# Seventy products of zeros among the first three head pairs, PSUM buffers for phi and its way back, and a split placed two units later

## The chip, the cores and the metric

The kernel runs on one core of one Trainium2 chip. The metric is the time of one execution on the device in microseconds (us). A core has TensorE (PE: matmuls and transposes, results go to PSUM), VectorE (DVE), ScalarE (ACT), GpSimd (POOL), SyncE (SP), which issues most DMAs here, and 16 DMA engines. Each engine works through its own instructions in order; between engines they wait on semaphores.

## The reference

Three layers, each fed by the one before:

```python
# attention: 4 batches, 8 heads, 576 tokens, 64 per head; blocks of 64
scores = scale * np.matmul(q, k.transpose(0, 1, 3, 2))
mask = block_i >= block_j
scores = np.where(mask, scores, -1000000000.0)
attn = softmax(scores)            # exp(s - max) / (sum + 1e-09)
out = np.matmul(attn, v)          # as x: 2304 tokens of 512
# a layer with a bend
h = x @ w_in                      # 512 -> 2048
g = np.where(pos, h, np.where(neg, 0.0, (h + beta) ** 2 / (4.0 * beta)))
x = g @ w_out                     # 2048 -> 512
# soft mixture: 8 experts of 4 slots
logits = x @ phi                  # 512 -> 32
d = softmax(logits, over tokens); slot_input = d.T @ x
slot_out[e] = np.maximum(slot_input[e] @ w1[e], 0.0) @ w2[e]
c = softmax(logits, over slots);  return c @ slot_out
```

## The kernel before

**Attention.** Sixteen units of work, one for each batch and pair of heads ("pair" 0 to 15). A string, PLAN, lists the steps of six overlapping pairs for one round; rounds follow each other, so it sets the order of instructions. For a pair and a group i of query rows (i = 4, 3, ... 0, two blocks of 128 rows each), `sc` i is six matmuls of scores into a PSUM tile of two banks (L120; L113 for i = 4), `mk` i adds the mask with two small matmuls (L126), `mx` takes the negative row maxima on DVE (L146, tile `nm`), `ex` the exponentials on ACT (L151, tile `pr`), `no` scales them on POOL (L163), `pt` transposes them on PE (L171), `pc` copies the result out (L254 on ACT, or DVE), and `pv` multiplies by the values (L189, L194). Score tiles have two buffers (pool `psc`), so `sc` of one group waits until ACT has read the group before the last. In this phase POOL, ACT and DVE also prepare the first seven tiles of `w_in` (READY).

**Split products.** `h = x @ w_in` is computed in three terms with both operands split into a high and a low part. A tile w of `w_in` takes a chain: raw data by DMA, `w_mul` on ACT (L460), four steps of `w_bits` on DVE (L466 to L469, tile `wab`), the cast of the high part on ACT (L254), then two steps on POOL (L484 and L485) that leave the low part in `w`. Inputs x are split by block of tokens: `split` casts on ACT (L409, `xh`) and subtracts on POOL (L412, `xl`).

**The layer after attention** (`Moe.run`). UNITS lists (block, tile) in order; unit k is twelve matmuls L538 into a tile `h` (pool `ptr`, tag "tr", three buffers; transposes of attention use the same group), followed by the bend: for even k below 18 three steps on ACT (L561, L562, L564), for odd k one on ACT (L559) and one on DVE (L572), then L573 on DVE for both, which reads `h` last and so frees it. The units here are k = 0 (block 1, tile 4), 1 (1, 5), 2 (1, 6), 3 (0, 7), 4 (1, 7), 5 (0, 8), 6 (1, 8), 7 (0, 9); w7 is needed at k = 3, w8 at 5, w9 at 7. In the loop, before unit k's matmuls, come `w_parts` of one weight (cast and POOL steps), `w_mul` and `w_bits` of another, and at k = 1 `parts[1]`, the second half of the split of block 2.

**The weight `w_out`, folded with phi.** The transposes `wo_turn` (L498), `wo_phi` (L507: 32 matmuls of a turned tile with `phi`, and an ACT copy to `y`, L511) and `wo_back` (L516: one transpose, and an ACT copy to `w2p`, L517) all write one bank, `aside[:, 1]`, the second bank of a tile kept from `psc`. There are four `phi` and four returns, in places that a planner lays (the four `phi` begin at 276.96, 298.80, 321.96 and 346.22 us); each stands after the third quarter of a unit's matmuls (`mid` in `h_unit`) or behind a unit.

**Tail.** Soft mixture and experts, with expert weights streamed in by DMAs whose issues wait for buffers. Here 25 products of zeros (`gap`, L1015) stand between dependent steps; 44 others (`warm`, L30) open the program.

Of the kernel before, what the change touches and what calls it, by code (L numbers as in the profile page):

```python
# [7 lines left out]
F32 = mybir.dt.float32  # L8
# [6 lines left out]
P = 128  # L15
# [223 lines left out]

FILL = ""  # L240
WARM = 44

# [3 lines left out]
def attention(e, tc, nb=4, wl=(1, 1 + 2 * READY)):  # L248
    nc = tc.nc
    e.ENG = ENG  # L250

    def copy(eng, dst, src):
        if eng == "A":
            nc.scalar.copy(dst, src)  # L254
        elif eng == "D":
            nc.vector.tensor_copy(dst, src)
        else:
            nc.gpsimd.tensor_scalar(out=dst, in0=src, scalar1=1.0, scalar2=1.0, op0=ALU.mult, op1=ALU.mult)
    e.copy = copy
    e.eng = lambda c: nc.vector if c == "D" else nc.gpsimd  # L260

    e.QD, e.pr, e.v_, e.acc = [], [], [], []
    for i in range(2):
        e.QD.append(e.apool.tile([P, 2, P], F32R, tag=f"QD{i}", bufs=1, name=f"QD{i}"))
        z = (nc.gpsimd, nc.vector)[i]
        z.memset(e.QD[i][0:64, :, 64:P].bitcast(F32), 0.0)
        z.memset(e.QD[i][64:P, :, 0:64].bitcast(F32), 0.0)
        e.pr.append([e.apool.tile([P, P * (b // 2 + 1)], F32, tag=f"pr{i}{b}", bufs=1, name=f"pr{i}{b}")
                     for b in range(9)])
        z.memset(e.pr[i][8][:, 576:640], 0.0)  # L270
        e.v_.append(e.apool.tile([P, 5, 2, 64], F32, tag=f"natv{i}", bufs=1, name=f"vn{i}"))
        z.memset(e.v_[i][64:P, 4], 0.0)
    for i in range(2):
        e.acc.append(e.apool.tile([P, 16, 2], F32, tag=f"acc{i}", bufs=1, name=f"ac{i}"))
        nc.vector.memset(e.acc[i], 1e-9)
    e.low = e.apool.tile([P, P], mybir.dt.bfloat16, tag="low", bufs=1, name="low")
    e.one = e.apool.tile([P, 64], mybir.dt.bfloat16, tag="one", bufs=1, name="one")
    nc.vector.memset(e.low, 0.0)
    nc.vector.memset(e.one, 1.0)
    for h in (0, 64):  # L280
        nc.vector.memset(e.low[h:h + 1, 0:64], -2.0 ** 127)
    pairs = [Pair(e, nc, b, p) for b in range(nb) for p in range(4)]
    n = len(pairs)
    plan = [(it - int(u[0]), u[1:]) for it in range(n + 6) for u in PLAN.split()]
    plan = [(i, u) for i, u in plan if ((i, int(u[2:])) in EARLY if u[0] == "h" and u[1] in "mxyzoa" else
                                        0 <= i < n if u[0] != "w" else wl[0] <= i < wl[1])]
    fill = [(int(u[0]), u[1:]) for u in FILL.split()]
    assert sorted(fill) == sorted(plan[:len(fill)])
    for i, u in fill + plan[len(fill):]:
        if u[0] == "h":  # L290
            e.moe.early(u[1], *EARLY[i, int(u[2:])])
        elif u[0] != "w":
            pairs[i].step(u)
        else:
            t, c = (i - wl[0]) // 2, slice((i - wl[0]) % 2 * 256, (i - wl[0]) % 2 * 256 + 256)
            if u == "w0" and c.start == 0:
                e.moe.w_raw(t)
            elif u == "w1":
                e.moe.w_mul(t, c)
                e.moe.w_bits(t, c)  # L300
            elif u == "w2":
                e.moe.w_parts(t, c, e.ENG["w"])
# [14 lines left out]
class Moe:  # L317
# [183 lines left out]

    def wo_phi(self, c):
        e, nc = self.e, self.nc
        ps = self.aside[:, 1]
        for kk in range(4):
            for i in range(4):
                nc.tensor.matmul(ps[32 * i:32 * i + 32, 0:P], e.phi[:, kk], self.wT[2 * c + i // 2][:, i % 2, kk],  # L507
                                 start=(kk == 0), stop=(kk == 3))
        self.drop(f"wT{4 * c}", f"wT{4 * c + 2}")
        wp = self.wp = e.y[:, 3]  # L510
        nc.scalar.copy(wp, ps[:, 0:P])  # L511

    def wo_back(self, c):
        e, nc = self.e, self.nc
        ps = self.aside[:, 1]
        nc.tensor.transpose(ps[:, 0:P], self.wp, e.ident)  # L516
        nc.scalar.copy(e.w2p[:, 4 * c:4 * c + 4].rearrange("p i s -> p (i s)"), ps[:, 0:P])  # L517

# [374 lines left out]
    def run(self):  # L893
        if not self.dry:
            d = Moe(Null(), Null(), self.live)
            d.home, d.w = dict(self.home), dict.fromkeys(range(READY), Null())
            d.xw = dict.fromkeys(self.xw, Null())
            d.xt = dict.fromkeys(self.xt, Null())
            d.g = dict.fromkeys(self.g, Null())
            d.run()  # L900
            self.plan, self.middle, self.bend = d.tape, d.middle, d.bend
            self.ends = {k: t for t, k in enumerate(d.tape) if isinstance(k, tuple)}
            self.cap = sum(self.CAP.values())
            self.tape = []
        self.gn, self.v, self.S = {}, {}, {}
        units = self.UNITS
        at, prep = self.plan_sides({u: k for k, u in enumerate(units)})
        e, nc = self.e, self.nc
        self.aside = e.psc.tile([P, 2, 512], F32, tag="sc", name="aside")
        self.lt = {1: self.aside[:, 0]}  # L910
        for i in range(READY, READY + 2):
            self.w_raw(i)
        self.w_mul(READY)
        self.w_bits(READY)
        parts = list(self.split(2))
        parts[0]()
        for k, (b, f) in enumerate(units):
            for i in [READY + n for n, p in enumerate(prep) if p == k - 1]:
                self.w_parts(i)
            for i in [READY + n for n, p in enumerate(prep) if p == k > 0]:  # L920
                self.w_mul(i)
                self.w_bits(i)
            if k == 1:
                parts[1]()
            for i in [READY + n for n, p in enumerate(prep) if max(p - 2, 0) == k and n > 1]:
                self.w_raw(i)
            self.h_unit(b, f, at.pop(-k, ()) if k else ())
            self.act_unit(b, f, "D" if k > prep[-1] or k < 18 and k % 2 else "A")
            for fn, *a in at.pop(k, []):
                (getattr(self, fn) if isinstance(fn, str) else fn)(*a)  # L930
            if k == 66:
                self.n4 = self.new([P, 4, 256], F32R, "n4")
                for i in range(4):
                    self.comb_parts(i)
            if k == 57:
                self.middle, self.spare = len(self.tape), 1
            if k > 29:
                self.feed()
        assert not at
        self.bend = len(self.tape)  # L940
        self.spare = 0
        self.chain()
        self.tail()
# [301 lines left out]
```

## Time and profile before

| what | value |
|---|---|
| median of 3 runs | 523.71 us (523.31 to 523.95) |
| the profiled execution | 523.28 us, of which 521.5 are the span of instructions |
| mean granted clock of PE | 0.98 of full speed |
| PE busy | 500.6 us, 96% |
| DVE, ACT, POOL busy | 331.6, 327.0, 203.9 us |
| moved by DMA | 91.01 MB, mean 175 GB/s |

The profile is one execution on the hardware. Busy times of PE are modelled at their ends, since matmuls are pipelined. "Idle before, releaser" names what ended the idle time ahead of an instruction. The granted clock is in parts of 2.4 GHz; 0.50 is 1.2 GHz. PEld is the loading of weights into PE, which overlaps with matmuls.

### The profile page before, as it was taken

The numbers are of one execution on the slowest core, as the hardware profiler recorded it, in microseconds if no ns is written. First come the engines' busy times: TensorE is split into PE (matmuls) and PEld (weight loads), VectorE is DVE, ScalarE is ACT, GpSimd is POOL, SyncE is SP. The second block draws the span as 40 slices with busy tenths as digits, with TensorE's granted clock in tenths as the row PEclk, the third lists the DMA queues.
The fourth block names the chain that finished last, engine by engine and source line by source line (L and its number), as shares of the span: only waits on it lengthen the run. The fifth ranks groups of instructions, "written<-read, shape, count | busy, mean of one in ns | idle before, by whom it ended". The sixth has DMA issues, their size and how long they took to land.

```text
span 521.5 us, 11780 instructions
## 1 busy us (share of the span) xinstructions
PE 500.6 (96%) x4504; PEld 384.5 (74%) x4504; DVE 331.6 (64%) x672; ACT 327.0 (63%) x734; POOL 203.9 (39%) x264
## 2 busy tenths in 40 slices
PE   6799999999999999899999999899999999999994
PEld 5678887888888887688887887788767978753453
DVE  6879988888887655888888545833463444431232
ACT  4889998888887645557787888643333535452131
POOL 3888997777777424744523212600002000000000
PEclk8789999999999999899999999999999999999998
DMA  6235334343321155111257865341075679979997
GB/s 204 92 95 167 115 99 142 88 125 98 91 52 29 53 163 215 53 43 61 101 168 236 288 235 184 110 154 41 5 277 175 222 253 412 391 237 373 411 412 308
DMA packets 42711, 91.01 MB, mean 175 GB/s; under 512 B 8736, under 2 KB 18080, under 8 KB 42656
## 3 DMA queue, kind: packets, MB, share of 16 engines
q1 hardware_dynamic: 42656, 90.26, 51.0%
q8 instruction: 36, 0.59, 0.4%
q14 instruction: 19, 0.16, 0.1%
HBM read 74.51 MB, written 14.68 MB: 171 GB/s over the span
## 4 chain that ended last, share of the span: by engine, by line
PE 81%; ACT 4%; DMA 3%; DVE 3%; issue 1%; POOL 1%; SPq 0%; ACTq 0%; DVEq 0%; POOLq 0%
PE h L538 33%; PE sc L120 7%; PE gn L593 5%; PE om L189 5%; PE s L658 3%; PE eh L1031 3%; PE ps_1p L171 2%; PE sc L113 2%; PE lt L613 2%; PE ps_2p L171 2%; PE ps_3p L171 2%; PE acc L1058 2%; PE om L194 2%; PE ps_0p L171 2%; DMA ew<-in_w2b_dram 1%
## 5 line engine op out<-in xcount | busy, mean ns | idle before, releaser
L538 PE MATMUL h<-xh,w 128*128 128x512 f32 (+1 forms) x384 | 115.2, 368 | 0.0
L538 PE MATMUL h<-xt,w 128*128 128x512 f32 x384 | 101.2, 408 | 1.6 <-POOL w L485 1.4
L163 POOL TENSOR_SCALAR pr<-pr,sm 128x512 f32<-128x512 f32 (+2 forms) x144 | 88.7, 633 | 24.7 <-DVE sm L158 23.0
L151 ACT ACTIVATE pr<-sc,nm 128x512 f32<-128x512 f32 (+2 forms) x144 | 78.3, 551 | 10.1 <-DVE nm L146 8.6
L538 PEld LDWEIGHTS h<-xt,w 128*128 128x128 f32 x384 | 69.5, 191 | 16.2 <-POOL w L485 2.7
L572 DVE SCALAR_TENSOR_TENSOR g<-g 128x512 f32<-128x512 f32 (+1 forms) x52 | 37.6, 724 | 65.6 <-ACT g L559 65.6
L538 PEld LDWEIGHTS h<-xh,w 128*128 128x128 f32 x384 | 69.0, 189 | 13.8 <-issue 3.8
L538 PE MATMUL h<-xl,w 128*128 128x512 f32 (+1 forms) x192 | 68.1, 355 | 0.0
L146 DVE TENSOR_REDUCE nm<-sc 128x2 f32<-128x1024 f32 (+1 forms) x64 | 52.3, 818 | 21.2 <-PE sc L126 20.9
L573 DVE TENSOR_TENSOR g<-h,g 128x512 f32<-128x512 f32 (+1 forms) x80 | 50.9, 636 | 15.8 <-ACT g L564 13.7
L559 ACT ACTIVATE g<-h,half 128x512 f32<-128x512 f32 (+1 forms) x52 | 32.3, 622 | 43.1 <-PE h L538 41.5
L120 PE MATMUL sc<-K,Q 64*128 64x512 f32 (+3 forms) x384 | 47.8, 363 | 3.7 <-ACT pr L151 2.7
L689 POOL TENSOR_TENSOR cn<-cn,cm 128x128 f32<-128x128 f32 (+1 forms) x5 | 1.9, 378 | 124.7 <-DVE cm L688 124.7
L254 ACT COPY gn<-gn 128x1024 f32<-128x1024 f32 x35 | 35.3, 1009 | 13.1 <-PE gn L593 12.7
L120 PEld LDWEIGHTS sc<-K,Q 64*128 64x128 f32 x384 | 30.2, 196 | 14.0 <-issue 5.6
L538 PEld LDWEIGHTS h<-xl,w 128*128 128x128 f32 x192 | 36.4, 189 | 3.8
L477 POOL TENSOR_TENSOR wab<-wab 128x512 f32<-128x512 f32 x16 | 21.0, 1312 | 44.0 <-DVE wab L469 23.3
L593 PE MATMUL gn<-ident,g 128*128 128x128 f32 x280 | 36.7, 274 | 0.2 <-ACT gn L254 0.2
L593 PEld LDWEIGHTS gn<-ident,g 128*128 128x128 f32 x280 | 31.7, 140 | 6.7 <-issue 2.1
L484 POOL TENSOR_TENSOR wab<-wab,w 128x256 f32<-128x256 f32 (+1 forms) x23 | 23.2, 1010 | 22.5 <-ACT w L254 21.3
L467 DVE SCALAR_TENSOR_TENSOR wab<-wab 128x512 uint32<-128x512 uint32 (+1 forms) x39 | 25.4, 651 | 10.0 <-ACT wab L460 6.6
L561 ACT ACTIVATE g<-h,half 128x512 f32<-128x512 f32 x28 | 19.3, 689 | 19.9 <-PE h L538 15.8
(226 smaller groups left out, 892.1 us busy)
## 6 DMA issues: line engine op xcount, KB each, us to landing
ew<-in_w_dram SPq DMA_DIRECT2D x32, 512.0 KB, 6.8
raw<-in_w_in_dram SPq DMA_DIRECT2D x16, 512.0 KB, 5.3
raw<-in_w_out_dram SPq DMA_DIRECT2D x16, 512.0 KB, 4.3
ew<-in_w2a_dram SPq DMA_DIRECT2D x16, 510.0 KB, 8.8
ew<-in_w2b_dram SPq DMA_DIRECT2D x16, 344.0 KB, 6.7
kn<-in_k_dram SPq DMA_DIRECT2D x16, 288.0 KB, 3.2
qn<-in_q_dram SPq DMA_DIRECT2D x16, 288.0 KB, 4.3
vn<-in_v_dram SPq DMA_DIRECT2D x16, 256.0 KB, 3.3
```

The source lines that it names most:

```text
L120: nc.tensor.matmul(sc[:, h, 0:n], self.Q[r, qa, 128 * i:128 * i + 128], self.K[r, ka, 0:n], start=(k == 0), stop=False)
L146: nc.vector.tensor_reduce(out=self.negm[:, 2 * i:2 * i + 2], in_=self.scs[i][:, :, 0:128 * (i + 1)], axis=AX.X, op=ALU.max, negate=True)
L151: self.nc.scalar.activation(pr, sc, AF.Exp, bias=self.negm[:, b:b + 1], accum_out=self.acc[:, b, 0:1])
L163: self.nc.gpsimd.tensor_scalar(out=pr, in0=pr, scalar1=self.sums[:, b:b + 1], scalar2=1.0, op0=ALU.mult, op1=ALU.mult)
L171: nc.tensor.transpose(ps[:, u * P:(u + 1) * P], self.pr[b][:, kc * P:(kc + 1) * P], e.ident)
L189: nc.tensor.matmul(om[64 * h:64 * h + 64, (t0 - ts[0]) * P:len(ts) * P], self.v[:, kc, h, :], self.PT[:, a:a + 2 * n - 1:2], start=(kc == ...
L254: nc.scalar.copy(dst, src)
L538: nc.tensor.matmul(ph[:, 0:n], w[:, wi, kk], self.x(b, kk, xi)[:, 0:n], start=(kk + m == 0), stop=(kk + m == 5))
L559: nc.scalar.activation(g, ph, AF.Relu, bias=e.half[:, 0:1], scale=0.5)
L572: nc.vector.scalar_tensor_tensor(out=g, in0=g, scalar=1.0, in1=g, op0=ALU.min, op1=ALU.mult)
L573: nc.vector.tensor_tensor(out=g, in0=ph, in1=g, op=ALU.max)
L593: nc.tensor.transpose(ps[:, j, i * P:(i + 1) * P], self.gt(b, f)[:, o:o + P], e.ident)
```

## The change

It does three things.

First, a table KEEP gives for ten `mk` steps of pairs 0, 1 and 2 a number of 128x128 products of zeros (bf16, the constant tile that `warm` uses too), 70 in all: 28 in pair 0, 27 in pair 1 and 15 in pair 2. They stand right behind the `mk` step on PE, write into a new tile of the "tr" group each, and nothing reads them.

Second, `wo_phi` and `wo_back` take a tile of the "tr" group each (`ph`, `bk`) and write there; `wo_turn` stays in `aside[:, 1]`.

Third, `parts[1]` is called at unit k = 3 where it was called at k = 1.

```diff
--- before.py
+++ after.py
@@ -239,6 +239,8 @@
 
 FILL = ""
 WARM = 44
+KEEP = {(0, "mk2"): 20, (0, "mk1"): 6, (0, "mk0"): 2, (1, "mk3"): 6, (1, "mk2"): 6, (1, "mk1"): 13, (1, "mk0"): 2,
+        (2, "mk3"): 5, (2, "mk2"): 5, (2, "mk1"): 5}
 
 
 
@@ -291,6 +293,10 @@
             e.moe.early(u[1], *EARLY[i, int(u[2:])])
         elif u[0] != "w":
             pairs[i].step(u)
+            if (i, u) in KEEP:
+                keep = e.ptr.tile([P, 512], F32, tag="tr", name=f"keep{i}{u}")
+                for _ in range(KEEP[i, u]):
+                    nc.tensor.matmul(keep[:, 0:P], e.zero, e.zero, start=True, stop=True)
         else:
             t, c = (i - wl[0]) // 2, slice((i - wl[0]) % 2 * 256, (i - wl[0]) % 2 * 256 + 256)
             if u == "w0" and c.start == 0:
@@ -501,7 +507,7 @@
 
     def wo_phi(self, c):
         e, nc = self.e, self.nc
-        ps = self.aside[:, 1]
+        ps = e.ptr.tile([P, 512], F32, tag="tr", name=f"ph{c}")
         for kk in range(4):
             for i in range(4):
                 nc.tensor.matmul(ps[32 * i:32 * i + 32, 0:P], e.phi[:, kk], self.wT[2 * c + i // 2][:, i % 2, kk],
@@ -512,7 +518,7 @@
 
     def wo_back(self, c):
         e, nc = self.e, self.nc
-        ps = self.aside[:, 1]
+        ps = e.ptr.tile([P, 512], F32, tag="tr", name=f"bk{c}")
         nc.tensor.transpose(ps[:, 0:P], self.wp, e.ident)
         nc.scalar.copy(e.w2p[:, 4 * c:4 * c + 4].rearrange("p i s -> p (i s)"), ps[:, 0:P])
 
@@ -920,7 +926,7 @@
             for i in [READY + n for n, p in enumerate(prep) if p == k > 0]:
                 self.w_mul(i)
                 self.w_bits(i)
-            if k == 1:
+            if k == 3:
                 parts[1]()
             for i in [READY + n for n, p in enumerate(prep) if max(p - 2, 0) == k and n > 1]:
                 self.w_raw(i)
```

Lines of the kernel after stand 2 lower from L239 on and 6 lower behind attention's loop (L484 is L490, L412 is L418, L498 is L504, and so on).

On POOL, from the first half of block 2's split to the third of the weights that follow. Before (`xl_3054` and `xl_3081` are the halves; `w_3076`, `w_3130` and `w_3175` are w7, w8 and w9):

```order
L412 TENSOR_TENSOR xl_3054<-xw_148,xh_3053 128x512 x2
L484 TENSOR_TENSOR wab_3047<-wab_3047,w_3076 128x512
L485 TENSOR_TENSOR w_3076<-wab_3047 128x512
L412 TENSOR_TENSOR xl_3081<-xw_149,xh_3080 128x512 x2
L484 TENSOR_TENSOR wab_3101<-wab_3101,w_3130 128x512
L485 TENSOR_TENSOR w_3130<-wab_3101 128x512
L484 TENSOR_TENSOR wab_3150<-wab_3150,w_3175 128x512
L485 TENSOR_TENSOR w_3175<-wab_3150 128x512
```

And after (in the same order w7, w8 and w9 are `w_3156`, `w_3205` and `w_3255`, the second half `xl_3210`):

```order
L418 TENSOR_TENSOR xl_3134<-xw_148,xh_3133 128x512 x2
L490 TENSOR_TENSOR wab_3127<-wab_3127,w_3156 128x512
L491 TENSOR_TENSOR w_3156<-wab_3127 128x512
L490 TENSOR_TENSOR wab_3176<-wab_3176,w_3205 128x512
L491 TENSOR_TENSOR w_3205<-wab_3176 128x512
L418 TENSOR_TENSOR xl_3210<-xw_149,xh_3209 128x512 x2
L490 TENSOR_TENSOR wab_3230<-wab_3230,w_3255 128x512
L491 TENSOR_TENSOR w_3255<-wab_3230 128x512
```

The second `xl` has gone from ahead of w8's two steps to behind them, ahead of w9's.

On ACT, from the cast of w7 to that of w8. Before:

```order
L254 CAST w_3076<-wab_3047 128x512
L409 CAST xh_3080<-xw_149 128x1024
L559 ACTIVATE g_4_3071<-h_5_3085,half 128x512
L460 ACTIVATE wab_3101<-raw_3045 128x512
L561 ACTIVATE g_6_3122<-h_6_3109,half 128x512
L562 ACTIVATE g_6_3122<-g_6_3122,unit 128x512
L564 ACTIVATE g_6_3122<-g_6_3122 128x512
L254 CAST w_3130<-wab_3101 128x512
```

And after:

```order
L256 CAST w_3156<-wab_3127 128x512
L565 ACTIVATE g_4_3151<-h_5_3160,half 128x512
L466 ACTIVATE wab_3176<-raw_3125 128x512
L567 ACTIVATE g_6_3197<-h_6_3184,half 128x512
L568 ACTIVATE g_6_3197<-g_6_3197,unit 128x512
L570 ACTIVATE g_6_3197<-g_6_3197 128x512
L256 CAST w_3205<-wab_3176 128x512
L415 CAST xh_3209<-xw_149 128x1024
```

The second cast `xh` has gone from ahead of the bend of unit 1 (its L559) to behind the cast of w8; the bends and `w_mul` (L460, then L466) keep their order among each other.

On PE, the matmuls between the first `phi` and the turn of a weight after it, with the semaphores on which they wait (each named by the engine that raises it). Before:

```order
L507 MATMUL aside<-wT_3552,phi 32x128 x2
L507 MATMUL aside<-wT_3612,phi 32x128 x2
L538 MATMUL h_4_3685<-xh_3080,w_1619 128x512
L538 MATMUL h_4_3685<-xl_3081,w_1619 128x512
L538 MATMUL h_4_3685<-xh_3080,w_1619 128x512
L498 MATMUL aside<-ident,wab_3618 128x128 [waits Activation_49,Pool_49]
L498 MATMUL aside<-ident,wab_3618 128x128 x3
L538 MATMUL h_5_3736<-xh_3053,w_1986 128x512 [waits DVE_49]
```

And after:

```order
L513 MATMUL ph_3775<-wT_3632,phi 32x128 x2
L513 MATMUL ph_3775<-wT_3692,phi 32x128 x2
L544 MATMUL h_4_3765<-xh_3209,w_1699 128x512
L544 MATMUL h_4_3765<-xl_3210,w_1699 128x512
L544 MATMUL h_4_3765<-xh_3209,w_1699 128x512
L504 MATMUL aside<-ident,wab_3698 128x128 [waits Pool_49]
L504 MATMUL aside<-ident,wab_3698 128x128 x3
L544 MATMUL h_5_3817<-xh_3133,w_2066 128x512 [waits DVE_49]
```

Nothing has moved here but the tile that is written; the turn (`aside`) no longer waits for ACT.

## Rows read from the trace of the kernel before

**Rows 1.** Page, part 1: TensorE's busy time and share of the span.

```profile
PE 500.6 (96%) x4504; PEld 384.5 (74%) x4504; DVE 331.6 (64%) x672; ACT 327.0 (63%) x734; POOL 203.9 (39%) x264
```

**Rows 2.** Waits of PE, 0-60 us: line, releaser, total us, times, longest.

```profile
PE sc L120 <- ACT pr L151: 2.7, 4, 1.5
```

**Rows 3.** Windows: PE, PEld, DVE, ACT, POOL busy (count), granted clock, DMA.

```profile
10.00:19.00 9.00, 7.07 (x38) 5.45 (x40) 6.41 (x15) 6.37 (x22) 7.06 (x9) 0.50 0.40 105
27.00:29.00 2.00, 2.00 (x13) 1.32 (x13) 1.62 (x2) 1.23 (x5) 2.00 (x4) 0.50 0.58 121
30.00:40.00 10.00, 10.00 (x113) 8.36 (x113) 8.28 (x20) 8.87 (x28) 8.49 (x13) 1.00 0.36 95
218.00:221.00 3.00, 3.00 (x8) 2.34 (x7) 1.38 (x3) 0.87 (x3) 2.56 (x2) 0.50 0.36 102
```

**Rows 4.** Timeline of PE: start us, length, line, operands, count, idle before.

```profile
11.07 1.78 PE L113 MATMUL sc<-K,QD 128*128 128x288 f32 x6 [2.20 <-ACT pr L151]
...
15.71 1.65 PE L120 MATMUL sc<-K,Q 64*128 64x512 f32 x6 [0.17 <-ACT pr L151]
...
25.00 0.55 PE L120 MATMUL sc<-K,Q 64*128 64x128 f32 x6 [1.47 <-ACT pr L151]
...
25.91 1.16 PE L120 MATMUL sc<-K,Q 64*128 64x512 f32 x6 [0.31 <-ACT pr L151]
...
31.13 1.04 PE L113 MATMUL sc<-K,QD 128*128 128x288 f32 x6
...
36.90 0.94 PE L120 MATMUL sc<-K,Q 64*128 64x512 f32 x6
```

**Rows 5.** Timeline of PE: products of zeros at both ends of the program.

```profile
0.99 4.87 PE L30 MATMUL warm<-warm 128*128 128x128 bf16 x44 [0.99 <-DVE warm L27]
...
510.10 0.72 PE L1015 MATMUL gap<-warm 128*128 128x128 bf16 x10
```

**Rows 6.** Timeline of ACT in the first pairs.

```profile
18.74 0.69 ACT L151 ACTIVATE pr<-sc,nm 128x512 f32<-128x512 f32 x1 [1.49 <-DVE nm L146]
...
30.54 0.58 ACT L254 COPY PT<-ps_1p 128x512 f32<-128x512 f32 x1 [0.58 <-PE ps_1p L171]
```

**Rows 7.** Timeline of PE around the late weight.

```profile
216.60 15.68 PE L538 MATMUL h<-xt,w 128*128 128x512 f32 x60 [1.43 <-POOL w L485]
```

**Rows 8.** Timeline of POOL in the same place.

```profile
208.81 3.18 POOL L412 TENSOR_TENSOR xl<-xw,xh 128x512 fp32r<-128x512 f32 x2
...
214.94 1.60 POOL L485 TENSOR_TENSOR w<-wab 128x512 fp32r<-128x512 f32 x1
...
220.03 1.28 POOL L485 TENSOR_TENSOR w<-wab 128x512 fp32r<-128x512 f32 x1
```

**Rows 9.** Timeline of ACT: first step of units 4, 6, 8.

```profile
214.36 0.69 ACT L561 ACTIVATE g<-h,half 128x512 f32<-128x512 f32 x1
...
223.52 0.69 ACT L561 ACTIVATE g<-h,half 128x512 f32<-128x512 f32 x1 [1.86 <-PE h L538]
...
228.96 0.69 ACT L561 ACTIVATE g<-h,half 128x512 f32<-128x512 f32 x1 [1.48 <-PE h L538]
```

**Rows 10.** Timeline of DVE: one weight step, beside POOL and alone.

```profile
210.94 1.59 DVE L467 SCALAR_TENSOR_TENSOR wab<-wab 128x512 uint32<-128x512 uint32 x1
...
216.94 0.69 DVE L467 SCALAR_TENSOR_TENSOR wab<-wab 128x512 uint32<-128x512 uint32 x1
```

**Rows 11.** Timeline of PE: transposes behind phi and its way back.

```profile
279.93 0.63 PE L498 MATMUL aside<-ident,wab 128*128 128x128 f32 x4 [0.99 <-ACT y L511]
...
330.68 0.63 PE L498 MATMUL aside<-ident,wab 128*128 128x128 f32 x4 [1.41 <-ACT w2p L517]
...
334.76 0.60 PE L498 MATMUL aside<-ident,wab 128*128 128x128 f32 x4
```

**Rows 12.** Timeline of DVE (first) and POOL there.

```profile
279.10 0.69 DVE L573 TENSOR_TENSOR g<-h,g 128x512 f32<-128x512 f32 x1
...
332.85 1.47 POOL L477 TENSOR_TENSOR wab<-wab 128x512 f32<-128x512 f32 x1
```

## The prediction

> **What bounds the kernel now.** I read the page first: TensorE (PE) is busy for 96% of the span [rows 1]. So the product work itself is the bound, and only two things can be saved: the few microseconds in which PE waits, and the stretches in which it works at half its clock. Matmuls do not change here except by 70 added ones.
>
> The waits of PE say how much there is of the first. In the first 60 us it waits four times, 2.7 us in all, at line 120, and once more, 2.20 us, at line 113, for ScalarE's (ACT's) exponentials `pr`, which release the score tiles [rows 2, 4]; later it waits 1.43 us for a split weight from GpSimd (POOL) [rows 7], and 0.99 and 1.41 us for two ACT copies out of the common bank `aside` [rows 11]. The three parts of the change sit exactly on these waits.
>
> The table by windows gives the second: the granted clock is 0.50 (1.2 GHz) from 10 to 19 us, 0.50 again from 27 to 29, 1.00 (2.4 GHz) from 30 to 40, and 0.50 once more from 218 to 221 [rows 3]. Each fall comes soon after a gap of PE: 2.20 us before 11.07, 1.47 us before 25.00 [rows 4], 1.43 us before 216.60 [rows 7]. From 25.91 [rows 4] to the gap near 215 I found no wait of PE, so whatever is gained by 26 us is kept there, unless another engine becomes late. The tail is fed by DMAs whose issues wait for buffers that PE's work frees; an earlier PE moves it along, and I give nothing back there.
>
> **Part 1, the products of zeros.** They remove no work; they fill PE's gaps so that the clock may stay up. Price of one: the same 128x128 product of zeros stands at the end of the program, at full clock, as 10 in 0.72 us, the start-up of the first among it, so at most 0.072 us each; the 44 opening ones took 4.87 us, 0.11 each, which I take as the price at half clock [rows 5]. Half of that is 0.055, my price at full clock. Seventy cost 3.9 us at full clock or 7.7 at half.
>
> What of that is covered: the 20 after pair 0's `mk2` (1.1 us at full clock) lie in the 2.20 us gap, the 6 after its `mk1` (0.33) in the next, smaller one, the 13 after pair 1's `mk1` (0.72) in the 1.47 us gap [rows 4]. If these gaps shrink, the cover shrinks as well. The other 31 include 6 + 6 in pair 1 (0.66 us), just ahead of transposes, and 15 in pair 2 (0.83 us), where PE waits for nothing, so those 15 are paid in full.
>
> What full clock gives back: the score group of 1.78 us takes 1.04 at full clock, the 1.65 one takes 0.94 (rows at 11.07 and 31.13, at 15.71 and 36.90) [rows 4]. Between 11 and 17.4 the path runs from PE's scores over VectorE's (DVE's) row maxima `nm` to ACT's exponentials: ACT waits 1.49 us for `nm` before 18.74 [rows 6]. On that path I count 0.34 us from the earlier release by ACT, about 0.2 from the shorter groups between, and 0.71 from the 1.65 us group: the exponentials of pair 1 start 1.25 us earlier. From there ACT is nearly without idle time to 25 us and sets PE's 25.00 start, so 1.25 is also about what pair 2's first scores (25.91) gain; with what small idle times ACT has between, 1.4. From 26.7 to 29.6 PE is busy at half clock and nothing else limits it: 2.9 us of half rate give back 1.45 us. Sum: 1.4 + 1.45 - 0.83 = 2.0; ACT's waits for `nm` in pair 2 also have to shrink, so I take **1.9 us**. Bounds: 2.5 above; below, a loss of 3.0 (the rival "half clock").
>
> The ten new tiles come from the three-buffer group that transposes and `h` also use. Two of them wait for an engine other than PE: that of pair 2's `mk1` for the ACT copy of `ps_1p` at 30.54, over at 31.1 [rows 6], while PE is still in the scores of tile 4 that began at 31.13 [rows 4]; that of pair 1's stands likewise. So this costs nothing; were the copies late, it would cost the delay itself.
>
> **Part 2, the second half of block 2's split, two units later.** Before, POOL runs `xl` (3.18 us) at 208.81, between the weight w7 and the weight w8; w8's two steps end at 216.54, and PE waits 1.43 us [rows 7, 8]. ACT's first step of a unit starts at 214.36, 223.52 and 228.96 us for the units k = 4, 6 and 8 [rows 9]: 9.16 us against 5.44 for the same work, so the stall and the half clock behind it cost 3.7 us. That is all that this part can give.
>
> Taking `xl` away from there lets DVE and POOL go faster. DVE's L467 took 1.59 us beside `xl` and 0.69 alone [rows 10]; POOL's L485 took 1.60 or 1.28 [rows 8]. So two-tensor steps of POOL and such steps of DVE take turns. Without `xl`, w8's chain comes about 2 us earlier: its L485 ends near 214.4, when PE needs it at about 214.9. No wait. But ACT's L559 of unit 1 no longer stands behind the cast `xh`, so DVE's L572 takes POOL's turn between w7's L484 and L485: w7 lands near 209.3, 0.45 us late.
>
> What is late next is w9. The moved `xl` runs behind w8's L485, from about 214.4 to 217.6, where DVE wants L466 and L467 for w9 (the second stood at 216.94 before [rows 10]). These slip to about 217.6 and 218.2, the cast to 218.9, POOL's pair to 219.3 and 221.1, and w9 lands at 221.9 to 222.4. PE needs it two units of 2.745 us after 214.9 (and the 0.45), at 220.4. So a gap of 1.4 to 2.0 us remains, one weight later. In total 1.85 to 2.45 lost, plus up to 1.7 if the clock falls, as it did after the gap of 1.43. Against 3.7 that is from -0.4 to +1.9; the kept gap is nearest in size to the one that brought the clock down, so I take a value under the middle, **+0.6 us**. Everything else on SP's and DVE's queues keeps its order.
>
> There is a rule on this: the Trainium skill, SBUF — State Buffer, section "SBUF: two separate sides", calls the port pair of the two engines an exclusive lock held for a whole instruction. The rows agree (1.59 against 0.69); by it the moved `xl` blocks w9's steps as a whole, as in the sum above.
>
> **Part 3, `phi` and its way back in PSUM buffers of their own.** Four `phi` (32 matmuls) and four returns leave the bank `aside`; the transposes L498 that follow need not wait for the ACT copies any more. Only two of the four places show a wait: 0.99 us at 279.93 (copy `y`), 1.41 us at 330.68 (copy `w2p`) [rows 11]. The new tiles take a place in the group of three, so the next `h` has to wait for the L573 of one unit later than before. First place: the transposes go at about 278.9, but `h` of the next unit waits for L573 of unit 3, over at 279.79 [rows 12]; before, it started 0.38 after the transposes' 279.93 [rows 11], and part of that 0.5 us comes back at the next `h`, whose L573 is late in the same way. I take 0.2. Third place: PE can go on 1.4 us sooner, but the transposes after the next unit need POOL's L477, ending at 334.32 [rows 12], where they started at 334.76 before [rows 11]: 0.4 of the 1.41 is left. The other two show no wait and stay at nothing. Sum **+0.6 us**, bounds -0.4 (a later `h` wait at all four, 0.1 each) to 2.4 (both waits whole).
>
> **Sum.** 1.9 + 0.6 + 0.6 = 3.1 us against the profiled execution of 523.28 (span 521.5, 1.8 around it): 520.2. The median of the runs is 523.71, 0.43 above the profiled one, so 520.6.
>
> **Rivals.**
> "The gap only moves": w9's gap is 2 us and the clock falls again (-0.4), and in the start the clock falls once, say in pair 0, where by the gaps less the products about 1.2 us stay idle, so that part 1 gives 1.1. With 0.6: 1.3, and 522.4. For it: every gap of 1.4 to 2.2 us brought the clock down [rows 3, 4, 7].
>
> "No new gap at w9": DVE's two steps slip in between the two halves of `xl`, and w9 is in time. Then part 2 gives its 3.7 less 0.45, and 1.9 + 3.2 + 0.6 = 5.7: 518.0. For it: L485 of w9 ended at 221.31 before [rows 8], 2 us ahead of the unit whose L561 [rows 9] follows it, so small slips need not show. With both `aside` waits whole as well, 516.2.
>
> "Half clock", slower: the products do not hold the clock. Then each costs 0.11, and those that no gap covers are paid: 12 in pair 1 and 15 in pair 2, 27 x 0.11 = 3.0 us; the clock costs what it did. The later parts give 0.6 + 0, so 523.7 + 2.4 = 526.1. It decides if the clock in 10 to 19 us still reads 0.50. Against it: the fall before 10 us came behind a gap of 2.20 us [rows 4], of which the 20 products fill half.
>
> "Transposes let the clock fall": with pair 1 running earlier, PE's work from 17 to 24 us is half transposes (24 of 128x128), the clock falls there, and about 2.5 us of the gain are lost: 523.1. Against it: from 30 to 40 us, with as many transposes, the clock stayed at 1.00 [rows 3]. There is such a rule: the Trainium skill, TensorE: Matmul & The Clock Gate, section "Part 4: PE-mode transpose", says that a transpose does not count as busy time in the same way; the row from 30 to 40 speaks against it here.
>
> "Nothing": the gaps were ACT's anyway and every saved step meets the next one; about 523.6.
>
> **How the numbers follow.** Chances: forecast 0.45 (own range 519.4 to 521.9), gap only moves 0.20, no new gap 0.16, that with whole `aside` waits 0.03, half clock 0.08, transposes 0.04, nothing 0.04. The range runs from 517.6, which takes in "no new gap", to 523.0, which takes in "gap only moves": 0.81. No change means within 0.2% (1.05 us), about what a measurement of this kernel can tell. Faster by more: 0.45 + 0.16 + 0.03 + 0.16 of "gap only moves" = 0.80; same: the rest of that, transposes, nothing = 0.12; slower 0.08.
>
> **What would show it.** Right: a clock near 1.00 from 9 to 30 us, pair 2's first scores near 24.4 and the first group of pair 3 near 35.0 instead of 36.90; no wait for w8, a wait for the weight two units on; PE's wait for `y` and `w2p` gone from L498. Wrong: a clock of 0.50 in 10 to 19; no wait for POOL at all around 220 (then it is faster than forecast); a new wait of `h` for DVE behind the `phi` matmuls; or PE waiting for ACT between 26 and 37, which would mean that the start's gain is not carried on.

## The result

The changed kernel takes 518.43 us (median of 4 runs, 517.44 to 519.80) against 523.83 us for the kernel before (4 runs, 523.31 to 524.22): a ratio of 0.9899, with a 95% interval from 0.9873 to 0.9926. A second set of runs gave 518.07 us (6 runs) against 524.10 (11 runs), ratio 0.9892 (0.9870 to 0.9913). Forecast were 520.6 us, a range of 517.6 to 523.0, and "faster". The time is in the stated range, though not in the forecast's own (519.4 to 521.9), and the sign is right; the gain is 5.4 to 6.0 us where 3.1 were forecast.

### The profile page after: what moved, and what is told of

The parts are those of the page before. It is cut to its first block, busy times and chain, and to the rows that moved or that the text cites. A ratio compares the mean times of both kernels' runs of the same rounds, so it can differ in the third digit from the quotient of the medians.

```text
span 517.2 us, 11928 instructions
## 1 busy us (share of the span) xinstructions
PE 498.4 (96%) x4574; PEld 383.4 (74%) x4574; DVE 332.2 (64%) x672; ACT 327.1 (63%) x734; POOL 204.8 (40%) x264
## 4 chain that ended last, share of the span: by engine, by line
PE 78%; DMA 7%; ACT 4%; DVE 4%; POOL 3%; issue 2%; SPq 1%; DVEq 0%; POOLq 0%; ACTq 0%
PE h L544 30%; PE sc L120 7%; PE gn L599 5%; PE om L189 5%; DMA gd<-g 4%; PE s L664 3%; PE eh L1037 3%; PE sc L113 2%; PE ps_2p L171 2%; PE ps_1p L171 2%; PE ps_3p L171 2%; PE lt L619 2%; PE ps_0p L171 2%; PE acc L1064 2%; PE om L194 2%
## 5 line engine op out<-in xcount | busy, mean ns | idle before, releaser
L544 PE MATMUL h<-xt,w 128*128 128x512 f32 x384 | 99.7, 403 | 1.4 <-POOL w L491 1.4
L544 PEld LDWEIGHTS h<-xt,w 128*128 128x128 f32 x384 | 68.3, 188 | 15.8 <-POOL w L491 3.1
L579 DVE TENSOR_TENSOR g<-h,g 128x512 f32<-128x512 f32 (+1 forms) x80 | 50.9, 636 | 14.7 <-ACT g L570 12.6
L120 PE MATMUL sc<-K,Q 64*128 64x512 f32 (+3 forms) x384 | 45.0, 347 | 3.1 <-ACT pr L151 1.6
L483 POOL TENSOR_TENSOR wab<-wab 128x512 f32<-128x512 f32 x16 | 21.0, 1314 | 43.8 <-DVE wab L475 21.8
L120 PEld LDWEIGHTS sc<-K,Q 64*128 64x128 f32 x384 | 28.5, 186 | 13.1 <-issue 5.3
L490 POOL TENSOR_TENSOR wab<-wab,w 128x256 f32<-128x256 f32 (+1 forms) x23 | 23.3, 1012 | 20.4 <-ACT w L256 19.2
```

Of the source, the lines that this page charges most:

```text
L120: nc.tensor.matmul(sc[:, h, 0:n], self.Q[r, qa, 128 * i:128 * i + 128], self.K[r, ka, 0:n], start=(k == 0), stop=False)
L544: nc.tensor.matmul(ph[:, 0:n], w[:, wi, kk], self.x(b, kk, xi)[:, 0:n], start=(kk + m == 0), stop=(kk + m == 5))
L579: nc.vector.tensor_tensor(out=g, in0=ph, in1=g, op=ALU.max)
```

## The profile after

The profiled execution took 518.95 us, of which 517.2 are its span (before: 523.28 and 521.5). Lines of this kernel stand 6 lower than before from the attention loop on. First PE's waits: line, releaser, total us, times, longest. The first two are of the first 60 us, the others of the rest.

```profile
PE sc L120 <- ACT pr L151: 1.6, 2, 0.8
PE sc L113 <- ACT pr L151: 1.5, 1, 1.5
...
PE h L544 <- POOL w L491: 1.4, 1, 1.4
PE h L544 <- POOL xl L418: 0.7, 1, 0.7
...
PE h L544 <- DVE g L579: 0.5, 1, 0.5
```

The four waits at line 120 [rows 2] have become two. The waits of the turns for ACT [rows 11] are gone. The 1.4 us for a weight is still there, and two smaller waits of `h` are new.

The windows answer to [rows 3] (busy us and count of PE, PEld, DVE, ACT, POOL, then granted clock, DMA share, GB/s):

```profile
10.00:19.00 9.00, 7.15 (x75) 5.75 (x75) 7.46 (x17) 7.76 (x27) 8.02 (x12) 1.00 0.40 129
27.00:29.00 2.00, 2.00 (x24) 2.00 (x21) 1.75 (x6) 1.88 (x8) 2.00 (x4) 1.00 0.91 260
30.00:40.00 10.00, 10.00 (x115) 8.10 (x113) 7.98 (x19) 9.04 (x30) 8.83 (x13) 1.00 0.45 122
218.00:221.00 3.00, 1.55 (x7) 0.98 (x6) 2.83 (x5) 1.90 (x4) 1.71 (x2) 1.00 0.52 172
```

All three stretches of half clock (0.50) read 1.00. The same 9 us that held 7.07 us of PE's work at half clock now hold 7.15 us at full clock. PE's timeline of the first pairs (start us, length, line, operands, count, idle before) answers to [rows 4]:

```profile
8.13 1.29 PE L299 MATMUL keep0mk<-warm 128*128 128x128 bf16 x20
10.91 1.03 PE L113 MATMUL sc<-K,QD 128*128 128x288 f32 x6 [1.49 <-ACT pr L151]
...
14.81 0.96 PE L120 MATMUL sc<-K,Q 64*128 64x512 f32 x6
...
23.08 0.55 PE L120 MATMUL sc<-K,Q 64*128 64x128 f32 x6 [0.75 <-ACT pr L151]
...
23.99 0.96 PE L120 MATMUL sc<-K,Q 64*128 64x512 f32 x6
...
34.67 0.94 PE L120 MATMUL sc<-K,Q 64*128 64x512 f32 x6
```

The gaps of 2.20 and 1.47 us are 1.49 and 0.75 now; the group of 1.65 us takes 0.96; the first scores of pair 2 start at 23.99 (before 25.91), those of pair 3 at 34.67 (before 36.90). These 2.2 us stay unchanged up to 208 us, as PE waits for nothing in between.

Around the weights (PE, then POOL, then the same DVE step for w8 and w9, then ACT's first step of the units 4, 6 and 8):

```profile
219.84 12.49 PE L544 MATMUL h<-xt,w 128*128 128x512 f32 x53 [1.45 <-POOL w L491]
```

```profile
212.03 3.18 POOL L418 TENSOR_TENSOR xl<-xw,xh 128x512 fp32r<-128x512 f32 x2
216.49 1.61 POOL L490 TENSOR_TENSOR wab<-wab,w 128x512 f32<-128x512 f32 x1 [1.28 <-ACT w L256]
218.19 1.60 POOL L491 TENSOR_TENSOR w<-wab 128x512 fp32r<-128x512 f32 x1
```

```profile
207.34 0.69 DVE L473 SCALAR_TENSOR_TENSOR wab<-wab 128x512 uint32<-128x512 uint32 x1
...
214.16 1.60 DVE L473 SCALAR_TENSOR_TENSOR wab<-wab 128x512 uint32<-128x512 uint32 x1
```

```profile
212.33 0.69 ACT L567 ACTIVATE g<-h,half 128x512 f32<-128x512 f32 x1 [0.92 <-PE h L544]
...
217.77 0.69 ACT L567 ACTIVATE g<-h,half 128x512 f32<-128x512 f32 x1 [0.19 <-PE h L544]
...
225.16 0.69 ACT L567 ACTIVATE g<-h,half 128x512 f32<-128x512 f32 x1 [1.47 <-PE h L544]
```

Units 4 to 6 take 5.44 us now (before 9.16), but units 6 to 8 take 7.39 (before 5.44) [rows 9]: the gap of 1.4 us has moved from w8 to w9, which lands at 219.79. The cause stands in the DVE rows: w9's step at 214.16 runs beside the moved `xl` (212.03 to 215.21) and takes 1.60 us, where w8's took 0.69. The clock did not fall behind the gap.

## The experiments

For the reading of their traces I took the start of the same matmul in each profile and subtracted it from its start in the first profile of before. So a row tells how many microseconds earlier (negative: later) a profile stands than that one, at the first scores (6.89 us), in pair 4 (41 us), behind the weights w8 and w9 (226 us), and behind the third phi (341 us).

| profile | first scores | 41 us | 226 us | 341 us | median, us |
|---|---|---|---|---|---|
| before, second profile | -0.18 | -3.08 | -1.50 | -2.21 | 523.5 to 524.1 |
| split_only | -0.31 | -1.77 | -0.23 | -0.12 | 523.26 |
| phi_only | -0.08 | -1.88 | -0.31 | 0.30 | 523.17 |
| keep_only | 0.62 | 2.52 | 4.12 | 5.12 | 519.29 |
| split_back | 0.17 | 2.07 | 2.04 | 3.44 | 519.29 |
| after, first profile | 0.67 | 2.22 | 3.80 | 4.47 | 518.43 |
| after, second profile | -0.56 | 0.46 | 2.01 | 3.03 | 518.07 |
| split_17 | 0.17 | 2.09 | 5.42 | 4.66 | 519.09 |
| split_spread | 0.47 | 2.37 | 5.20 | 6.78 | 517.19 |
| spread_two_pairs | -0.09 | 0.95 | 3.77 | 3.93 | 518.29 |
| keep_pair0 | 0.12 | 1.48 | 3.02 | 4.37 | 519.56 |
| fill_gaps | 0.05 | 2.55 | 5.39 | 5.10 | 516.97 |

The first column follows the arrival of the first load, and differs by over 1 us between executions of one kernel: in the two profiles of the changed one (0.67 and -0.56) ACT's first step waits 3.47 and 4.70 us for the DMA of `qn`.

**keep_only: the products of zeros alone.**

From the changed kernel (the same line for `bk`):

```diff
-        ps = e.ptr.tile([P, 512], F32, tag="tr", name=f"ph{c}")
+        ps = self.aside[:, 1]
...
-            if k == 3:
+            if k == 1:
                 parts[1]()
```

> The kernel before with the seventy products of zeros alone. My theory: the clock stays at 1.00 from 9 to 30 us, pair 3's first scores start near 34.7 instead of 36.90, and the 2.2 us are carried to the end; the late weight w8 near 216 and both waits behind phi and its way back stay as before. So 2.2 us faster than before. Rival 'the first microseconds were luck': the earlier start of the first scores (0.67 us) in the changed kernel's profile was a difference between executions, and only about 1.5 us are left.

Measured: 519.29 us, ratio 0.9909 (0.9882 to 0.9936), so 4.6 us: twice the expected. The start is as expected (pair 4 is 2.52 us earlier). The rest came in a place that this kernel does not touch:

```profile
214.08 18.18 PE L544 MATMUL h<-xt,w 128*128 128x512 f32 x78 [1.43 <-POOL w L491]
```

```profile
217.00:221.00 4.00, 4.00 (x19) 3.31 (x18) 3.39 (x6) 2.46 (x5) 2.17 (x2) 1.00 0.38 131
```

PE's timeline shows the same gap of 1.43 us before w8's unit as [rows 7], and the window behind it reads 1.00, not 0.50. That alone is worth 1.60 us (4.12 - 2.52). So the half clock at 218 us in the first profile of before does not follow from the gap alone.

**split_only and phi_only: the other two parts alone.** One has `parts[1]` at k = 3 and nothing else, the other the two tiles `ph` and `bk` and nothing else.

> The kernel before with the second half of the split moved from unit 1 to unit 3 alone. My theory: w8 is in time, w9 is about 1.4 us late, and the gain is 0.6 to 1.9 us by whether the clock falls after that gap; in the changed kernel it did not, so 1.6 us. Rival 'the clock was saved by something else': the gap of 1.4 us brings the clock down here as it did before, and the gain is 0 to 0.3 us.

> The kernel before with phi and its way back in PSUM tiles of their own alone. My theory: the waits of the transposes for the two ACT copies go, in the first place a wait of h for DVE of about 0.5 us and in the third a wait for POOL of about 0.7 to 0.9 us come in their stead; 0.6 to 0.7 us faster. Rival 'both waits go whole': 2.4 us faster.

Measured: 523.26 us, ratio 0.9989 (0.9970 to 1.0008), and 523.17 us, ratio 0.9987 (0.9966 to 1.0008): 0.6 and 0.7 us by medians, neither resolved. In split_only the gap is at w9, the clock stays up behind it, and 1.54 us are gained up to 226 us, as my theory said. But phi_only, with the gap at w8, gains 1.57 us in the same stretch. Both start 1.8 us later than the first profile of before: without products of zeros their clock was down for longer in the first 35 us. So that profile had a lucky start and an unlucky clock at 218 us, and both had gone into my sums.

**before_again: a second profile of the kernel before.**

> The kernel before once more, for a second profile. Theory 'chance': the gap of 1.4 us before w8's unit is there, with the clock behind it up or down by chance, and the half clock of the first 35 us is of another length than in the first profile (in 10 to 19 us 0.50, then between 3 and 7 us more of it). Rival 'place': the same stretches as in the first profile, 10 to 19.7, 26.7 to 29.6 and 217.8 to 221 us.

Measured: 525.34 us for this one execution. Its windows:

```profile
10.00:19.00 9.00, 6.56 (x36) 4.94 (x36) 6.54 (x14) 6.60 (x21) 7.07 (x9) 0.50 0.33 84
...
29.00:32.00 3.00, 3.00 (x16) 2.30 (x16) 2.17 (x5) 1.45 (x4) 3.00 (x5) 0.50 0.92 223
32.00:35.00 3.00, 3.00 (x15) 3.00 (x14) 1.90 (x6) 2.88 (x7) 0.95 (x3) 0.50 0.19 74
...
218.00:221.00 3.00, 1.57 (x8) 1.09 (x7) 2.83 (x5) 1.73 (x4) 1.60 (x1) 1.00 0.03 8
```

```profile
219.70 12.50 PE L538 MATMUL h<-xt,w 128*128 128x512 f32 x53 [1.43 <-POOL w L485]
```

"Chance" holds. The gap at w8 is there with 1.43 us, and the clock stays up behind it. At the start it is down until 35 us, where the first profile had 1.00 from 30 on [rows 3]; this costs 3.08 us up to pair 4.

**after_again: a second profile of the changed kernel.** It was to tell whether the clock falls behind w9's gap by chance or never; expected were 4.3 to 5.5 us under before. Measured: 6.0 us, the second set of runs above. The gap at w9 is there (1.44 us) and the clock stays up, so this question stays open. But the first pair shows something else:

```profile
10.31 2.31 PE L299 MATMUL keep0mk<-warm 128*128 128x128 bf16 x20
12.38 1.58 PE L113 MATMUL sc<-K,QD 128*128 128x288 f32 x6
13.89 0.62 PE L120 MATMUL sc<-K,Q 64*128 64x256 f32 x6
```

The twenty products take 2.31 us (1.29 in the first profile), the score group 1.58 (1.03), the next group 0.62 in both. So by the durations PE worked at half clock up to about 13.6 us, although the windows of this profile read 1.00 there. Net of the first scores it has gained 1.02 us in pair 4, less than any other profile with the seventy products.

**split_back: the changed kernel with the split back at unit 1.**

```diff
-            if k == 3:
+            if k == 1:
                 parts[1]()
```

> The changed kernel with the second half of the split back at unit 1: the products of zeros and the tiles of phi stay. Theory 'the move is worth nothing': the gap of 1.4 us is before w8's unit in place of w9's, the clock mostly stays up behind either, and the time is that of the changed kernel within 0.5 us (some 5.5 us under before). Rival 'the move is worth its 1.6 us': the clock falls behind w8's gap as it did in the first profile of before, and it is 1.5 us slower than the changed kernel.

Measured: 519.29 us, ratio 0.9911 (0.9881 to 0.9940), against 518.07 and 518.43 with the move. In its profile the clock does fall behind the gap at w8:

```profile
215.00:218.00 3.00, 3.00 (x10) 2.33 (x9) 2.29 (x4) 0.62 (x1) 1.63 (x2) 0.57 0.12 14
```

With the gap at w8 the clock fell in 2 of 5 profiles (before, split_back; not in before_again, phi_only, keep_only). With the gap at w9 it fell in none of 4 (after twice, split_only, keep_pair0). Between both sets everything else in the stretch is equal: +1.6 us where the clock stays, 0 where it falls. Whether w9 is the safer place or the four were lucky stays open; by medians the move is worth about 1 us, and the intervals allow anything from a loss of 1 to a gain of 3.

**split_17: the split behind the last weight of w_in.** The changed kernel with `if k == 17`.

> The changed kernel, with the second half of the split at unit 17, behind the last weight of w_in, instead of unit 3. My theory (DVE's weight steps and POOL's subtraction of the split take turns, and there is no room for both within one weight's period): no weight is late any more, the gap of 1.4 us before w9's unit goes, and it is 1.4 us faster than the changed kernel, about 7 us faster than before. Rival 'w9 is late by its own chain': the gap stays, no gain. Rival 'the split is needed earlier': a new wait of block 2's first unit for xl at about 255 us, of 1 to 3 us.

Measured: 519.09 us, ratio 0.9900 (0.9873 to 0.9928): nothing gained over the changed kernel. The gap at w9 did go (5.42 us earlier at 226, against 3.80). But 2.5 us are lost between 255 and 275 us, where `w_out`'s chain starts; 1.6 us of it are waits of the turns:

```profile
257.41 0.66 PE L504 MATMUL aside<-ident,wab 128*128 128x128 f32 x4 [0.78 <-POOL wab L483]
261.11 0.66 PE L504 MATMUL aside<-ident,wab 128*128 128x128 f32 x4 [0.27 <-POOL wab L483]
265.07 0.63 PE L504 MATMUL aside<-ident,wab 128*128 128x128 f32 x4 [0.57 <-ACT wT L256]
```

So in each of the three places tried, xl of 3.18 us delayed the weight that came next: w8, w9 or the first of `w_out`. My theory got the gap right, and I had not named the victim behind it.

**split_spread: the subtraction in four pieces.** `xl` of the second half is issued as four pieces of 256 columns, at k = 3, 5, 7 and 9:

```diff
-            if k == 3:
-                parts[1]()
+            if k in (3, 5, 7, 9):
+                self.split_piece(2, 1, (k - 3) // 2)
```

Piece 0 also makes the cast `xh`.

> The changed kernel, with POOL's subtraction of the second half of the split cut into four pieces of 256 columns (0.8 us each by 3.18 / 4), one behind each of the weights w8 to w11, where the changed kernel has all of it behind w8. My theory (within one weight's period DVE and POOL have about 1.2 us to spare, so 0.8 fits and 3.2 does not): no weight is late by more than 0.3 us, the gap of 1.4 us before w9 goes, and it is 1.4 us faster than the changed kernel. Rival 'each piece delays its weight': four small gaps, 1 to 1.4 us in sum, and no gain.

Measured: 517.19 us, ratio 0.9866 (0.9844 to 0.9888). The gap before w9 in PE's timeline, and a piece on POOL behind that weight:

```profile
218.43 13.89 PE L555 MATMUL h<-xt,w 128*128 128x512 f32 x59 [0.39 <-POOL w L502]
```

```profile
218.33 0.93 POOL L429 TENSOR_TENSOR xl<-xw,xh 128x256 fp32r<-128x256 f32 x1
```

Of 1.45 us, 0.39 are left, and the later pieces cost nothing that the trace shows: 2.83 us are gained from 41 to 226 us, where the changed kernel gains 1.58. A piece of about 0.9 us fits beside a weight, one of 3.18 us does not. By medians this is 0.9 us under the changed kernel in the same set of runs (518.07); the intervals overlap.

**spread_two_pairs and keep_pair0: fewer products of zeros.** The first is split_spread without the fifteen in pair 2, the second the changed kernel with the 28 in pair 0 alone.

> The kernel with the split in four pieces, and without the fifteen products of zeros in pair 2. My theory: in pair 2 PE waits for nothing, so that these fifteen are paid in full and hold nothing; 0.8 us faster than with them, 2.2 us faster than the changed kernel, and the clock at 1.00 from 26 to 40 us. Rival 'they hold the clock through the transposes of pair 2': the clock falls to 0.50 somewhere in 26 to 32 us, and it is 0 to 1 us slower than with them.

> The changed kernel with the 28 products of zeros in pair 0 alone; the 42 in pairs 1 and 2 are left out. My theory: the clock stays at 1.00 through pair 0; in pair 1 the gap before the last scores (0.75 us in the changed kernel) grows to about 1.5 us and brings the clock down between 23 and 30 us in a part of the executions, as 1.47 us did before, which costs up to 1.5 us, against 0.8 us saved in pair 2: from 0.8 us faster to 0.7 us slower than the changed kernel. Rival 'pair 0 decides all': the clock stays at 1.00, and it is 0.8 us faster.

Measured: 518.29 us, ratio 0.9894 (0.9874 to 0.9915), and 519.56 us, ratio 0.9920 (0.9895 to 0.9945). By medians spread_two_pairs was 1.1 us slower than split_spread, not 0.8 faster (the intervals overlap); keep_pair0 was 1.5 us slower than the changed kernel in the same set of runs, where 0.8 faster to 0.7 slower was expected. My theory of the fifteen fell: in the profile without them the clock fell. The window of spread_two_pairs and two rows of PE's timeline:

```profile
26.00:30.00 4.00, 3.87 (x21) 3.17 (x22) 2.55 (x5) 2.35 (x7) 3.77 (x7) 0.57 0.78 213
```

```profile
23.47 0.55 PE L120 MATMUL sc<-K,Q 64*128 64x128 f32 x6 [0.86 <-ACT pr L151]
...
28.22 2.21 PE L171 MATMUL ps_1p<-ident,pr 128*128 128x128 f32 x12
```

The clock is down from about 26 to 30 us, though PE is busy 3.87 of these 4 us; twelve transposes take 2.21 us there. The last longer gap was 0.86 us, at 22.6 to 23.5; one of 0.23 us, for POOL's `pr`, ends at 26.13. The gap alone does not bring the clock down: split_spread, with the fifteen, has the same gap and keeps 1.00.

```profile
26.00:30.00 4.00, 4.00 (x40) 3.73 (x39) 3.52 (x10) 3.68 (x12) 3.62 (x7) 1.00 0.76 218
```

```profile
22.93 0.55 PE L120 MATMUL sc<-K,Q 64*128 64x128 f32 x6 [0.86 <-ACT pr L151]
```

In keep_pair0 the clock stayed up through pair 0, as expected, and the same stretch was at half clock (0.60 in 26 to 30 us), behind a gap of 1.78 us.

**fill_gaps: the products moved into the gaps.** From split_spread: 16 behind pair 0's mk1, 24 behind pair 1's mk1, none in pair 2.

```diff
-KEEP = {(0, "mk2"): 20, (0, "mk1"): 6, (0, "mk0"): 2, (1, "mk3"): 6, (1, "mk2"): 6, (1, "mk1"): 13, (1, "mk0"): 2,
-        (2, "mk3"): 5, (2, "mk2"): 5, (2, "mk1"): 5}
+KEEP = {(0, "mk2"): 20, (0, "mk1"): 16, (0, "mk0"): 2, (1, "mk3"): 6, (1, "mk2"): 6, (1, "mk1"): 24, (1, "mk0"): 2}
```

> The split in four pieces, and the products of zeros where PE waits in pairs 0 and 1 instead of in pair 2: 16 (before 6) behind pair 0's mk1, 24 (before 13) behind pair 1's mk1, none in pair 2. Theory 'the gap brings the clock down': with the gaps of 0.8 us in pairs 0 and 1 filled, the clock stays at 1.00 through pair 2, and it is 0.8 us faster than the split in four pieces with all seventy. Rival 'the stretch of transposes and small scores in pair 2 is itself too thin': the clock falls between 26 and 30 us as without the fifteen, and the time is about that of spread_two_pairs, 1.1 us slower than the split in four pieces.

Measured: 516.97 us, ratio 0.9868 (0.9838 to 0.9897). Same stretch, and the gap in pair 1:

```profile
26.00:30.00 4.00, 3.96 (x34) 3.59 (x35) 3.79 (x8) 3.54 (x11) 3.74 (x6) 1.00 0.81 211
```

```profile
23.36 0.55 PE L120 MATMUL sc<-K,Q 64*128 64x128 f32 x6 [0.27 <-ACT pr L151]
```

With the gap filled from 0.86 to 0.27 us the clock stays at 1.00 through pair 2, without one product there. Pair 0's gap was filled too, from 0.81 to 0.25 us; which of the two counts was not separated. Net of the first scores' time it is 2.50 us earlier in pair 4, 0.6 more than split_spread (2.37 - 0.47). In the median the expected 0.8 us does not show. In its profile PE waits 1.4 us at 314 us for ACT's copy `gn`, which came late because ACT had waited for a DMA that stores `g` in DRAM:

```profile
311.06 0.69 ACT L577 ACTIVATE g<-h,half 128x512 f32<-128x512 f32 x1 [3.54 <-DMA gd<-g]
```

In the other profiles PE waits there 0.4 us at most; why it is longer here is not shown. split_spread and fill_gaps, at 0.9866 and 0.9868, are by medians the fastest of the kernels that ran, about 0.2 to 0.3% under the changed one; the intervals overlap with its own.

## Why the prediction was right or wrong

**Part 1 (1.9 us): right in the mechanism, undersized.** The clock stayed at 1.00 from 9 to 40 us in five of the six profiles with the seventy products; in the sixth (after, second profile) PE ran at half clock up to about 13.6 us and at full clock from there. Between the first two profiles the term is near: 2.2 us, of which 0.67 is the earlier first load; without it 1.25 us are gained up to pair 2 (1.4 forecast), and 0.31 from there to pair 3 (1.45 - 0.83 forecast). But the kernel before loses more in other executions. Net of the first scores, the four profiles without products stand at 0, -2.90, -1.46 and -1.80 in pair 4, those with them at 1.55, 1.02, 1.90, 1.90, 1.92 and 1.90: on the mean -1.54 and 1.70, so the products are worth 3.2 us; alone they gave 4.6 by medians (3.4 to 6.2 by the interval). The failed step is reading the length of the half clock from one execution as if it belonged to the program. The sentence that from 26.7 to 29.6 PE lost 1.45 us was about true of that execution (it was down until 29.9); in before_again the clock was down up to 35 us.

The products do not hold the clock in every execution either. The mean granted clock of each execution is on record: 0.976 to 0.990 in the 23 of the kernel before that ran beside keep_only (median 0.980), 0.988 to 0.997 in the 33 with the seventy products (median 0.994). The profiles among these in which the windows show no fall read 0.994 to 0.997; nine executions read 0.991 or less, among them the slowest of four of the five kernels. By my estimate 0.004 less is 4 us at half clock (0.004 x 517 / 0.5). Where the clock fell in them is not on record, and a late start like that of after_again does not show in this mean.

**That the fifteen products in pair 2 were paid in full for nothing** was the wrong half of the same step: they cost about 0.6 us (fill_gaps against split_spread in pair 4, which differ in the gaps as well), and without them the clock fell. What they seem to make up for is the gap before them: where fill_gaps filled it, they could be spared. Each of these two readings rests on one profile. The mean clocks of the other executions do not bear them out: three of the five of split_spread read 0.991, five of the six of spread_two_pairs 0.993 to 0.996. So how often the fifteen hold the clock is not shown.

**Part 2 (+0.6 us): the place was right, the size a matter of chance.** w8 in time, w9 late: forecast 1.4 to 2.0 us of gap, w9 landing at 221.9 to 222.4; measured 1.45 us, w9 landing at 219.79, which is 222.0 when the 2.2 us of the start are added. Even the 0.18 us lost at w7 showed (2.22 at 208 us, 2.04 at 211; 0.45 forecast). The price of 3.7 us for the stall and the half clock was near: where both are gone, in split_17, 3.3 us are gained from 41 to 226 us. What was wrong was counting the fall of the clock behind w8 (about 1.6 us) as a property of that gap: of five gaps of that length at w8, three left the clock up. Since the gap did not shrink (1.43 and 1.45 us), the move saves no PE wait at all. What it saves, if anything, is the chance of the fall.

**Part 3 (+0.6 us): right, as far as it can be told.** The first place:

```profile
274.94 0.60 PE L504 MATMUL aside<-ident,wab 128*128 128x128 f32 x4
276.05 0.50 PE L544 MATMUL h<-xh,w 128*128 128x512 f32 x1 [0.51 <-DVE g L579]
```

The turn waits no more, and the next `h` waits 0.51 us for DVE's L579 instead of the turn's 0.99 for ACT, as forecast. (The prediction also lists such a wait among the signs of being wrong, though its own sum counts on it; the sum was right.) At the third place PE's wait, and POOL's step behind which it stands, are

```profile
328.84 0.50 PE L544 MATMUL h<-xl,w 128*128 128x512 f32 x1 [0.73 <-POOL xl L418]
```

```profile
325.81 2.98 POOL L418 TENSOR_TENSOR xl<-xw,xh 128x512 fp32r<-128x512 f32 x2 [1.71 <-ACT xh L415]
```

so POOL takes over, as forecast, but one step earlier than I had it: `h` needs the low part of block 3's split, which ends at 328.79, before the turn needs L483 behind it. The stretch from 270 to 341 us gains 0.65 us. Other executions gained 0.61 (phi_only), 1.0 (after, second profile), 1.4 (split_back) and 1.6 us (split_spread) there, and keep_only, without this part, 0.97, before_again -0.8: what else differs between executions moves this stretch by as much as the part is worth. The wait of ACT for the store of `g` near 311 us, for one, is 0.69 us in split_spread and 3.54 in fill_gaps. On the mean the nine profiles with this part gain 0.86 us there (-0.3 to 1.6) and the four without it 0.08 (-0.8 to 1.0): near the forecast, and not resolved.

**The sum.** 3.1 us forecast, 5.4 to 6.0 measured. The parts alone give 4.6 + 0.6 + 0.7 = 5.9 us by medians, so they add up. The surplus is part 1's, 3.2 to 4.6 in place of 1.9; parts 2 and 3 have about their forecast size by medians, and neither is resolved alone. That the stated range holds the time is luck in part: it reached down to 517.6 for the rival "No new gap at w9" (518.0), and that gap is there.

**The rivals.** "The gap only moves" came true for the gap and not for the clock. "No new gap at w9" was the price of another kernel, split_spread. "Half clock" was off: the clock reads 1.00 in 10 to 19 us. "Nothing" is off by the time. "Transposes let the clock fall" is refuted as it stood, since the changed kernel keeps the clock up from 17 to 24 us:

```profile
17.00:24.00 7.00, 6.15 (x73) 5.31 (x69) 6.66 (x18) 6.88 (x20) 5.76 (x10) 1.00 0.49 160
```

In spread_two_pairs busy transposes and scores behind a gap of 0.86 us did not prevent the fall. The rule that stood beside it (the Trainium skill, TensorE: Matmul & The Clock Gate, Part 4: PE-mode transpose) is neither shown nor refuted by that.

## What to carry to other kernels

Half clock behind short gaps differed here between executions of one kernel: before pricing a change that is to keep the clock up, take two or three profiles of the kernel before, price the mean, and look at the mean granted clock of every execution, not only of the profiled one. Put the products of zeros into the gaps, where PE would wait anyway, rather than into the busy stretch behind them (0.6 us dearer here, by one profile). A long step that runs beside a tight chain, on one of its engines or slowing its steps (1.60 against 0.69 us), delayed whichever link came next in each of three places; cut it so that each piece fits into the slack of one link.

## What the runs showed of the hardware

After gaps of the same length, 1.43 us, before the same instruction, the granted clock of PE fell to 0.50 in two profiles and stayed at 1.00 in three; the two executions of the kernel before are one of each. In the first pairs, where gaps of 0.2 to 2.2 us follow each other, it fell in all four profiles without products of zeros, and ended at 29.9, 32.2, 33.7 and 35 us by the windows. After a gap of 0.86 us the clock fell at about 26 us in spread_two_pairs; after gaps of 0.86 (split_spread) and 0.87 us (keep_only), with five products behind three of the score groups that followed, it stayed.

The time at which the clock first comes up differs too: in the first profile of the changed kernel the 44 opening products took 3.95 us and the first pairs ran at full clock, in the second they took 4.87 us and PE was at half clock up to about 13.6 us.

Two executions of one binary have their first scores 1.2 us apart (0.67 and -0.56), as far as ACT's wait for the first load is longer (3.47 and 4.70 us).

POOL's subtraction of 256 columns takes 0.92 to 0.93 us in three of four pieces of split_spread (1.19 in the first), that of 512 about 1.59 (3.18 for two): half the columns cost 0.58 of the time.
